# Sign and factor of the converted weights: two GpSimd multiplies against one on VectorE

## The chip, the core and the metric

The kernel runs on one core of a Trainium2 chip. A core has a matrix engine (TensorE, "PE" in the profile, its weight loads "PEld"), a vector engine (VectorE, "DVE"), an activation engine (ScalarE, "ACT"), a general engine (GpSimd, "POOL") and SyncE ("SP"), which here only issues transfers. Every engine works through its own list of instructions in order; a semaphore makes an instruction wait for another engine. The metric is the device time of one execution in microseconds (us).

## The reference

Top-k attention over 8 batches and 8 heads, with 576 positions and a head width of 64, followed by a block with a layer norm and two matrix products. Only the 32 largest scores of each row are kept:

```python
scores = scale * np.matmul(q, k.transpose(0, 1, 3, 2))
kth = np.partition(scores, -top_k, axis=-1)[..., -top_k:-top_k + 1]
scores = np.where(scores >= kth, scores, -1e9)
attn = softmax(scores)                 # written out in the reference
x = attn @ v                           # then (B,H,S,D) -> (B, S, H*D)
xn = (x - mean) / sqrt(var + 1e-6) * g_ln
out = x + maximum(xn @ w_ch1, 0) @ w_ch2
```

The weights w_ch1 (512 x 2048) and w_ch2 (2048 x 512) come in 64-bit floating point, so the kernel reads each of them as two 32-bit words and makes a 32-bit float of them itself; all else is 32-bit.

## The kernel before, in words

**Units and steps.** The attention is cut into 160 units: 128 rows of queries of a pair of heads (or 64 left-over rows), with all 576 keys. The main loop (lines 1263 to 1418) has one step per unit. In step n, VectorE picks the 32nd largest score of unit n. TensorE makes the scores of unit n+2, and ScalarE copies them out of PSUM. For unit n-1, whose threshold is there, ScalarE makes a mask (L532), GpSimd subtracts the scores from it (L535) and ScalarE takes the exponential (L543). The weighted values and the matrix products of finished blocks of rows fill TensorE in between.

**Selection.** `halve` (L447) folds a unit's 576 scores into the larger (L461) and the smaller (L462) of each pair of halves. `select(u, i)` for i = 0 to 3 takes the eight largest (MAX8, L483) of the larger half and replaces them by a very small number (MATCH_REPLACE8, L469); `select(u, 1)` also takes the eight largest of the smaller half (L475). After `select(u, 3)`, the last maximum, the threshold is known. In the kernel before, `halve` of the next unit follows the last maximum.

**Weights.** A `Piece` (L123) is 128 x 512 weights: 16 pieces of w_ch1, and 16 of w_ch2. It is fetched by SyncE (L148, 512 KB), and split (L150): ScalarE takes the absolute value of the upper word (L164), GpSimd clamps it (L165), ScalarE scales the lower word (L166) and takes the sign (L169); for w_ch1 GpSimd multiplies the row's factor from `gcol` into the sign (L171). In the next step VectorE shifts the bits of the upper word left by three (L177), GpSimd adds the lower word (L183) and multiplies by the sign (L185), which writes the finished weight.

**When pieces are converted.** `batches` says which pieces are split in which step: four ahead of step 0, one in each of steps 0 to 7, none in step 8, one in step 9, two in each step from 10 to 18, and the last one in step 19. `join_weights` makes the adds and multiplies a step later: at the end of the step up to step 8, where it also finishes one of the first four pieces, and near its start, behind the masks, from step 9 on. `weights` issues the fetches and the splits, from step 9 on at the end of the step. `ready` keeps the step in which a piece was finished.

**Matrix work.** A block of rows is given to the queue `todo` when its attention is done (the first in step 9). `fill` takes as much from it, eight times in a step, as `slot` allows: while weights are converted (`CONVERTING`), what VectorE's planned time of the step leaves beside TensorE's, and later an even share of what is open. An item whose weights are not ready is left for a later step. The order of all instructions is written out by this program; no scheduler changes it. Scores, transposes and values share five PSUM buffers ("ps"), matrix products have three ("mm").

Of the kernel before, what the change touches and what calls it, by code (L numbers as in the profile page):

```python
# [10 lines left out]
ALU = mybir.AluOpType  # L11
FP32 = mybir.dt.float32
# [17 lines left out]
def compute(  # L30
# [12 lines left out]
    nc = tc.nc  # L43
# [4 lines left out]
    NC, NF = DM // P, DFF // P  # L48
# [65 lines left out]
    half, gcol = columns[:, 0:J], columns[:, J : J + NC]  # L114
# [8 lines left out]
    class Piece:  # L123
# [26 lines left out]
        def split(self):  # L150
            i = self.i
            high = self.raw[:, :, 1].bitcast(FP32)
            if i < 3 * NC:
                self.size = hpool.tile([P, DM], U32, tag="h", name="size")[:]
                self.low = wt_rows[:, i % 8]
                homes = ((opool, "o"), (opool, "o"), (rpool, "r"), (rpool, "r"), (xtpool, "xT"))
            else:
                self.size = wt_rows[:, 2 * i % 8].bitcast(U32)
                self.low = wt_rows[:, (2 * i + 1) % 8]
                homes = ((opool, "o"), (opool, "o"), (rpool, "r"))  # L160
            pl, tag = homes[i % len(homes)]
            self.sign = pl.tile([P, DM], FP32, tag=tag, name="sign")
            size_f = self.size.bitcast(FP32)
            nc.scalar.activation(size_f, high, AF.Abs)  # L164
            nc.gpsimd.tensor_scalar(size_f, size_f, HIGH_MAX, HIGH_MIN, ALU.min, ALU.max)  # L165
            nc.scalar.activation(  # L166
                self.low, self.raw[:, :, 0], AF.Copy, bias=2.0, scale=2.0**-51
            )
            nc.scalar.activation(self.sign[:], high, AF.Sign)  # L169
            if self.i < NF:  # L170
                nc.gpsimd.tensor_scalar(  # L171
                    self.sign[:], self.sign[:], gcol[:, self.c : self.c + 1], 1.0,
                    ALU.mult, ALU.mult,
                )

        def shift(self):
            nc.vector.tensor_scalar(  # L177
# [3 lines left out]
        def join(self):  # L181
            size = self.size
            nc.gpsimd.tensor_tensor(size, size, self.low.bitcast(U32), ALU.add)  # L183
            size = size.bitcast(FP32)
            nc.gpsimd.tensor_tensor(self.dst, size, self.sign[:], ALU.mult)  # L185
            ready[self.i] = now[0]


# [12 lines left out]
    batches = {}  # L201
    queue = list(pieces)
    for n in range(-1, NF + 4):
        count = 4 if n < 0 else 1 if n < NF // 2 else 0 if n == NF // 2 else 1 + (n > 9)
        batches[n], queue = queue[:count], queue[count:]
    batches = {n: x for n, x in batches.items() if x}
    assert not queue
# [3 lines left out]
    def weights(n, phase):  # L211

        now, coming = batches.get(n, []), batches.get(n + 1, [])
        if phase == 0:
            for x in coming if n < LATE else []:
                x.fetch()
            for x in now[0::2] if n < LATE else []:
                x.split()  # L220
        elif phase == 1:
            for x in now if n >= LATE else now[1::2]:
                x.split()
            for x in coming if n >= LATE else []:
                x.fetch()

    def join_weights(n):
        for x in batches.get(n - 1, []):
            x.join()
# [8 lines left out]
    def pop():  # L238
        kind, cost, run, may = todo.pop(0)
        assert not may or may()  # L240
        owed[0] -= cost
        run()
# [30 lines left out]
    def fill(least=0):  # L273
        tick[0] += 1
        loads.settle(LOAD_AGE)
        sends.settle(SEND_AGE)
        ends_later.settle(END_AGE)
        fetch_forms(FETCH_AGE)
        owed[0] = min(owed[0] + share[0], 6.0)
        while todo and (not todo[0][3] or todo[0][3]()):  # L280
            if owed[0] < todo[0][1] / 2 and least <= 0:
                break
            least -= 1
            pop()
# [162 lines left out]
    def halve(u):  # L447

        nt = len(u.tiles)
        u.lo = lopool.tile([P, 2, HALF], FP32, tag="lo", name="lo")
        u.hi = hi_homes[u.i % 2]
        sides = int(doubt is not None)
        u.low, u.body = (sides * LOWS + HALF, sides * LOWS) if doubt is None or u.i // 2 % 2 else (0, LOWS)
        a, b = u.sc[:, 0:nt, 0:HALF], u.sc[:, 0:nt, HALF:S]
        lo, hi = u.lo[:, 0:nt], u.hi[:, 0:nt, u.body : u.body + HALF]  # L460
        nc.vector.tensor_tensor(hi, a, b, ALU.max)  # L461
        nc.vector.tensor_tensor(lo, a, b, ALU.min)  # L462

    def select(u, i):

        nt = range(len(u.tiles))

        def replace(m, t, x):
            nc.vector.match_replace(x, m[:, t, :], x, LOWEST)  # L469

        if i == 1:
            for r in range(low_rounds):
                o = u.low + 8 * r
                for t in nt:
                    nc.vector.max(u.hi[:, t, o : o + 8], u.lo[:, t])  # L475
                if r < low_rounds - 1:
                    for t in nt:
                        replace(u.hi[:, :, o : o + 8], t, u.lo[:, t])
        r0, width = (min(u.low, u.body), HALF + LOWS) if i > 1 else (u.body, HALF)
        pl = brief_small if i in (1, 2) else small  # L480
        m = pl.tile([P, 2, 8], FP32, tag=f"m{i}", name=f"m{i}")
        for t in nt:
            nc.vector.max(m[:, t, :], u.hi[:, t, r0 : r0 + width])  # L483
        if i < TOP_K // 8 - 1:
            for t in nt:
                replace(m, t, u.hi[:, t, r0 : r0 + width])
        if i == 0:
            u.top = m
        u.thr = m
# [47 lines left out]
    def weigh(u, t):  # L537
        g = u.group
        if g.den is None:
            g.den = denpool.tile([P, 2 * J + 1], FP32, tag="den", name="den")  # L540
        col = 2 * u.qt + t
        u.weighed += 1
        nc.scalar.activation(  # L543
            u.e[:, t], u.e[:, t], AF.Exp, bias=u.bias[:, t : t + 1], scale=-scale,
            accum_out=g.den[:, col : col + 1],
        )
        if u.rest:
            den = g.den[:, 2 * J : 2 * J + 1]
        elif u.weighed == 2 and u is [x for x in g.units if not x.rest][-1]:
            whole = [qt for qt in g.qts if qt < J]  # L550
            den = g.den[:, 2 * whole[0] : 2 * whole[-1] + 2]
            g.sums = den
        else:
            return
        nc.scalar.activation(den, den, AF.Copy, bias=DEN_EPS)
# [170 lines left out]
    class Block:  # L726
# [163 lines left out]
        def seven(self):  # L890
# [47 lines left out]
            def evacuate(k):  # L938
# [16 lines left out]
                def join():  # L955
# [8 lines left out]
                    if k == 5:  # L964
                        self.finish(0)

                joined[k] = sums_later.add(join)
                self.ends.append(joined[k])

# [86 lines left out]
    def fetch_forms(age):  # L1056
        if done(formed[0]):
            free = 4 + sum(tick[0] - x >= age for x in used)
            while fetched[0] < min(free, 8 * (len(blocks) - PLAIN)):
                fetch_form()  # L1060
# [96 lines left out]
    def at(i):  # L1157
        return units[i] if 0 <= i < N else None
# [104 lines left out]
    for n in range(END):  # L1263
# [8 lines left out]
        u, nxt, mk = at(n), at(n + 1), at(n - 1)  # L1272
# [34 lines left out]
            brings.pop(n)()  # L1307
        if u:
            select(u, 0)
        for x in batches.get(n - 1, []) if n else []:  # L1310
            x.shift()
        if n > NF // 2:
            join_weights(n)
        if quick:
            for den in recips.pop(n):
                nc.vector.reciprocal(den, den)
# [58 lines left out]
            parts[1]()  # L1375
        if u:
            select(u, 2)
        for blk, i in rows_of.pop(n, []):
            blk.stats(i)
        for blk in gives.get(n - 2, []):  # L1380
# [11 lines left out]
        if mk and len(mk.tiles) > 1 and mk.i >= EARLY:  # L1392
            weigh(mk, 1)
        fill()
        if u:
            select(u, 3)
        if nxt:
            halve(nxt)
        if n == 0:
            for x in batches[-1]:  # L1400
                x.shift()
            for x in batches[-1][:2]:
                x.join()
        weights(n, 1)
        if 0 < n <= NF // 2:
            join_weights(n)
            for x in batches[-1][n + 1 : n + 2]:
                x.join()
        if g and not quick and g.job.hp == NHP - 1:
            for qt in g.qts:  # L1410
                if qt < J:
# [17 lines left out]
@with_exitstack  # L1429
def kernel(  # L1430
    ctx: ExitStack,
    tc: tile.TileContext,
    *operands: bass.AP,
):
    nc = tc.nc
    doubt = ctx.enter_context(tc.tile_pool(name="doubt", bufs=1)).tile(
        [1, 1], I32, tag="doubt", name="doubt"
    )
    compute(tc, *operands, low_rounds=1, doubt=doubt[:])
    again = nc.values_load(  # L1440
        doubt[:], min_val=0, max_val=1,
        skip_runtime_bounds_check_because="a comparison's result",
    )
    with tc.If(again > 0):
        compute(tc, *operands, low_rounds=2, doubt=None)
# [31 lines left out]
```

## Time and profile before

| | us |
|---|---|
| median of the runs (lowest to highest) | 1571.86 (1570.28 to 1573.63) |
| profiled execution | 1571.11 |
| its span | 1569.2 |
| TensorE busy | 1469.0 |
| VectorE busy | 1363.4 |
| ScalarE busy | 1083.8 |
| GpSimd busy | 981.2 |

The page gives busy times, then the span in 40 equal slices of 39 us with the busy share in tenths. A group's row has its line, engine and operation, the tiles, their shapes and the count; behind the first bar the busy time in us and the mean of one in ns; behind the second the idle time of the engine in front of it, with what ended it. A row of the timeline begins with the start and the duration in us. A duration includes the time in which an instruction that has begun is held up. VectorE's and ScalarE's instructions overlap a little, so that the next starts up to 0.1 us before the end of one.

### The profile page before, as it was taken

What the parts mean: (1) busy time and instruction counts of PE and PEld (TensorE: products, weight loads), DVE (VectorE), ACT (ScalarE), POOL (GpSimd) and SP (SyncE); (2) the same over time, 40 slices, a digit from 0 to 9 for tenths busy, and PEclk for the clock granted to TensorE, in tenths of its full rate; (3) what the DMA queues carried; (4) which work ended last, traced back from release to release, by engine and by line L of the source; (5) the groups of instructions that cost most, each with busy time, mean ns of one, the idle gap of its engine ahead of it and who ended that gap; (6) DMA issues with size and microseconds to landing.
All of it is one profiled execution on the core that took longest, in us unless ns stands there. A gap on an engine that the chain in (4) does not pass through costs nothing. (4 is left out here: it accounts for less than half of the span.)

```text
span 1569.2 us, 27215 instructions
## 1 busy us (share of the span) xinstructions
PE 1469.0 (94%) x8046; PEld 1108.0 (71%) x8046; DVE 1363.4 (87%) x3873; ACT 1083.8 (69%) x3081; POOL 981.2 (63%) x1318
## 2 busy tenths in 40 slices
PE   4568889999999999999999999999999998999997
PEld 3346446566787677778777777777777776788886
DVE  7997999899979998999988999999999999768000
ACT  6978887786777767767768676768676776555421
POOL 6968995747465565756566647474746475737524
PEclk9779989999999999999999999999999999999999
DMA  6623551466728865577754687657677557454511
GB/s 170 167 85 97 137 139 53 124 178 181 226 83 194 202 208 153 168 199 153 216 148 134 174 200 197 173 150 191 175 201 206 162 164 208 121 166 125 150 35 50
DMA packets 374774, 245.60 MB, mean 157 GB/s; under 512 B 255956, under 2 KB 343512, under 8 KB 374616
## 3 DMA queue, kind: packets, MB, share of 16 engines
q1 hardware_dynamic: 371048, 243.17, 57.6%
q8 instruction: 67, 1.10, 0.3%
q10 hardware_dynamic: 3568, 0.59, 0.3%
q14 instruction: 91, 0.75, 0.2%
HBM read 166.14 MB, written 77.53 MB: 155 GB/s over the span
## 5 line engine op out<-in xcount | busy, mean ns | idle before, releaser
L535 POOL TENSOR_TENSOR e<-e,sc 128x576 f32<-128x576 f32 x288 | 416.0, 1462 | 453.8 <-ACT e L532 392.9
L819 PE MATMUL hps<-xT,w 128*128 128x256 f32 x2304 | 542.2, 384 | 2.4 <-ACT xT L781 2.4
L819 PEld LDWEIGHTS hps<-xT,w 128*128 128x128 f32 x2304 | 423.0, 191 | 82.2 <-issue 27.2
L483 DVE MAX8 m<-hi 128x8 f32<-128x296 f32 (+1 forms) x1152 | 471.3, 444 | 1.2
L469 DVE MATCH_REPLACE8 hi<-m,hi 128x288 f32<-128x288 f32 (+1 forms) x864 | 377.0, 441 | 0.0
L979 PE MATMUL ops<-w,h 128*128 128x256 f32 x1280 | 304.8, 383 | 1.4 <-ACT o L944 1.4
L979 PEld LDWEIGHTS ops<-w,h 128*128 128x128 f32 x1280 | 233.6, 190 | 44.3 <-issue 13.5
L419 ACT COPY sc<-scps 128x288 f32<-128x288 f32 x576 | 188.5, 402 | 78.5 <-POOL e L535 56.2
L543 ACT ACTIVATE e<-e,m 128x576 f32<-128x576 f32 x288 | 225.1, 784 | 14.6 <-POOL e L535 12.5
L532 ACT ACTIVATE e<-sc,m 128x576 f32<-128x576 f32 x288 | 209.4, 769 | 0.0
L842 ACT ACTIVATE h<-hps 128x512 f32<-128x512 f32 x144 | 86.7, 602 | 114.1 <-PE hps L819 113.5
L577 DVE STREAM_TRANSPOSE sc<-e 128x1152 f32<-128x1152 f32 x87 | 118.8, 1366 | 52.5 <-ACT e L543 46.3
L669 PE MATMUL av<-pt,vb 128*64 128x256 f32 (+2 forms) x1280 | 148.8, 376 | 9.5 <-DMA pt<-turned 7.7
L462 DVE TENSOR_TENSOR lo<-sc 128x576 f32<-128x576 f32 (+1 forms) x160 | 136.1, 850 | 0.0
L461 DVE TENSOR_TENSOR hi<-sc 128x576 f32<-128x576 f32 (+1 forms) x160 | 130.0, 812 | 3.0 <-ACT sc L419 3.0
L669 PEld LDWEIGHTS av<-pt,vb 128*64 128x64 f32 x1280 | 81.6, 140 | 66.4 <-issue 17.1
L438 PE MATMUL scps<-kT,late_qT 64*128 64x288 f32 (+3 forms) x832 | 121.7, 410 | 0.2 <-ACT pt L618 0.2
L979 PE MATMUL ops<-wt,s 128*128 128x256 f32 x512 | 119.4, 383 | 0.0
L475 DVE MAX8 hi<-lo 128x8 f32<-128x288 f32 x288 | 117.5, 443 | 0.0
L438 PE MATMUL scps<-kT,qT 64*128 64x288 f32 x512 | 92.6, 460 | 23.5 <-DVE qT L366 8.0
L606 PE MATMUL tp<-ident,e 128*128 128x128 f32 x456 | 74.2, 290 | 39.9 <-ACT e L543 28.9
L979 PEld LDWEIGHTS ops<-wt,s 128*128 128x128 f32 x512 | 94.7, 190 | 17.3 <-issue 4.4
(111 smaller groups left out, 1793.5 us busy)
## 6 DMA issues: line engine op xcount, KB each, us to landing
turned<-sc SPq DMA_DIRECT2D x87, 576.0 KB, 4.2
pt<-turned SPq DMA_DIRECT2D x348, 144.0 KB, 3.2
w<-forms SPq DMA_DIRECT2D x128, 256.0 KB, 4.7
vb<-in_v_dram SPq DMA_DIRECT2D x80, 288.0 KB, 4.2
raw<-in_moe_w_ch_dram SPq DMA_DIRECT2D x32, 512.0 KB, 4.5
kT<-kept SPq DMA_DIRECT2D x48, 288.0 KB, 3.7
kept<-kT SPq DMA_DIRECT2D x32, 288.0 KB, 3.6
kqin<-in_k_dram SPq DMA_DIRECT2D x116, 72.0 KB, 2.6
```

The costliest lines, as they stand in the source:

```text
L419: nc.scalar.copy(u.sc[:, t, s * HALF : (s + 1) * HALF], u.made[s][t][:, 0:HALF])
L438: nc.tensor.matmul(ps[i * R : i * R + ql, o : o + width], qT[r, q0 : q0 + ql], kT[r, k0 : k0 + width], start=True, stop=True,)
L461: nc.vector.tensor_tensor(hi, a, b, ALU.max)
L462: nc.vector.tensor_tensor(lo, a, b, ALU.min)
L469: nc.vector.match_replace(x, m[:, t, :], x, LOWEST)
L483: nc.vector.max(m[:, t, :], u.hi[:, t, r0 : r0 + width])
L532: nc.scalar.activation(u.e[:, t], u.sc[:, t], AF.Relu, bias=u.edge[:, t : t + 1], scale=-STEEP)
L535: nc.gpsimd.tensor_tensor(u.e[:, t], u.e[:, t], u.sc[:, t], ALU.subtract)
L543: nc.scalar.activation(u.e[:, t], u.e[:, t], AF.Exp, bias=u.bias[:, t : t + 1], scale=-scale, accum_out=g.den[:, col : col + 1],)
L669: nc.tensor.matmul(av[h * D : (h + 1) * D, 0 : g.nq], vb[:, h * (J + 1) + c, :], heads_of(g, h, 0, g.nq // 32)[:, :, c], start=(c == 0), s ...
L819: nc.tensor.matmul(ps[0][:, side * N : (side + 1) * N], w1[:, c, f * P : (f + 1) * P], self.xT[:, c, 0:N], start=(c == 0), stop=(c == NC - 1),
L979: nc.tensor.matmul(bank[name][:, 0:Q], a(j), rhs, start=first and j == 0, stop=(j == G - 1), skip_group_check=not first,)
```

## The change

The factor and the sign are no longer multiplied in by GpSimd: a new function `sign_it` makes one VectorE operation of both, (size x factor) x sign, and writes the finished weight. It comes after `select(u, 2)` of the step behind the split. The four pieces ahead of step 0 are shifted, added and multiplied in step 0 in place of steps 0 to 3. From step 4 on two pieces are split in a step, and the last two in step 15 in place of one in step 19. `halve` of the next unit moves in front of `select(u, 3)`, in all steps.

```diff
             nc.scalar.activation(self.sign[:], high, AF.Sign)
-            if self.i < NF:
-                nc.gpsimd.tensor_scalar(
-                    self.sign[:], self.sign[:], gcol[:, self.c : self.c + 1], 1.0,
-                    ALU.mult, ALU.mult,
-                )
...
         def join(self):
             size = self.size
             nc.gpsimd.tensor_tensor(size, size, self.low.bitcast(U32), ALU.add)
-            size = size.bitcast(FP32)
-            nc.gpsimd.tensor_tensor(self.dst, size, self.sign[:], ALU.mult)
+
+        def sign_it(self):
+            factor = gcol[:, self.c : self.c + 1] if self.i < NF else 1.0
+            nc.vector.scalar_tensor_tensor(
+                self.dst, self.size.bitcast(FP32), factor, self.sign[:], ALU.mult, ALU.mult
+            )
             ready[self.i] = now[0]
...
-        count = 4 if n < 0 else 1 if n < NF // 2 else 0 if n == NF // 2 else 1 + (n > 9)
+        count = 4 if n < 0 else 1 if n < 4 else 2
...
-        for x in batches.get(n - 1, []) if n else []:
+        for x in batches.get(n - 1, []):
             x.shift()
-        if n > NF // 2:
-            join_weights(n)
+        join_weights(n)
...
         if u:
             select(u, 2)
+        for x in batches.get(n - 1, []):
+            x.sign_it()
...
+        if nxt:
+            halve(nxt)
         if u:
             select(u, 3)
-        if nxt:
-            halve(nxt)
-        if n == 0:
-            for x in batches[-1]:
-                x.shift()
-            for x in batches[-1][:2]:
-                x.join()
         weights(n, 1)
-        if 0 < n <= NF // 2:
-            join_weights(n)
-            for x in batches[-1][n + 1 : n + 2]:
-                x.join()
```

## The prediction

> **What bounds the kernel now.** I read the page's busy shares and its 40 slices first, then a table of stretches, then the groups of VectorE and GpSimd in the stretch that the change touches, and last single steps in the timeline.
>
> ```profile
> span 1569.2 us, 27215 instructions
> PE 1469.0 (94%) x8046; PEld 1108.0 (71%) x8046; DVE 1363.4 (87%) x3873; ACT 1083.8 (69%) x3081; POOL 981.2 (63%) x1318
> ...
> PE   4568889999999999999999999999999998999997
> ...
> DVE  7997999899979998999988999999999999768000
> ...
> POOL 6968995747465565756566647474746475737524
> ```
> ```profile
> core 0: us, PE busy (x) PEld busy (x) DVE busy (x) ACT busy (x) POOL busy (x), PEclk, DMA share, GB/s
> 40.00:80.00 40.00, 23.18 (x121) 15.57 (x121) 38.27 (x103) 36.18 (x99) 38.67 (x35) 0.72 0.59 162
> ...
> 160.00:200.00 40.00, 33.12 (x137) 17.46 (x134) 39.82 (x101) 35.56 (x92) 35.85 (x33) 0.91 0.58 152
> 200.00:240.00 40.00, 33.47 (x133) 17.22 (x132) 39.76 (x103) 32.87 (x87) 36.36 (x35) 0.89 0.46 117
> ```
> ```profile
> 240.00:1345.00 1105.00, 1083.79 (x6180) 820.48 (x6180) 1067.97 (x3084) 801.53 (x2349) 667.62 (x940) 1.00 0.64 171
> ```
>
> The run has two regimes. From 240 us on TensorE is busy 98% (1083.8 of 1105), whatever VectorE does. Up to 240 us, the stretch in which the weights are converted, TensorE has holes (23 of 40 us busy, then 33), while VectorE and GpSimd are both full: 38.3 and 38.7 of 40, later 39.8 and 36. The matrix work queued per step is planned and stays the same within about a microsecond from step 22 on (so the order of the two kernels' instructions has it), so an engine change in the first 240 us is worth what it does to the moment at which step 20 ends. After it, TensorE is the limit and hands a delay or a gain through to the end.
>
> In the conversion stretch the groups are these (11.32 us is the first halving, 238.18 us the end of step 20's last maximum):
>
> ```profile
> L462 DVE TENSOR_TENSOR lo<-sc 128x576 f32<-128x576 f32 x21 | 25.3, 1204 | 0.0
> L461 DVE TENSOR_TENSOR hi<-sc 128x576 f32<-128x576 f32 x22 | 24.4, 1110 | 3.0 <-ACT sc L419 3.0
> L177 DVE TENSOR_SCALAR wt<-wt 128x512 uint32<-128x512 uint32 x20 | 18.9, 973 | 9.3 <-POOL wt L165 9.3
> ...
> L177 DVE TENSOR_SCALAR size<-size 128x512 uint32<-128x512 uint32 x12 | 6.4, 543 | 3.6 <-POOL size L165 3.6
> ```
> ```profile
> L185 POOL TENSOR_TENSOR w<-wt,sign 128x512 f32<-128x512 f32 x20 | 27.9, 1394 | 1.6
> L183 POOL TENSOR_TENSOR wt<-wt 128x512 uint32<-128x512 uint32 x20 | 27.0, 1350 | 0.0
> L171 POOL TENSOR_SCALAR sign<-sign,columns 128x512 f32<-128x512 f32 x16 | 17.0, 1065 | 3.4 <-ACT sign L169 1.6 <-ACT m L495 0.8
> L165 POOL TENSOR_SCALAR wt<-wt 128x512 f32<-128x512 f32 x20 | 15.9, 804 | 11.4 <-ACT wt L164 11.1
> ...
> L185 POOL TENSOR_TENSOR w<-size,sign 128x512 f32<-128x512 f32 x12 | 15.9, 1322 | 0.9
> ```
>
> VectorE's own rows hide a loss. Its instructions on two tensors take 0.75 us when GpSimd is quiet and up to twice that beside it; a pair of shifts takes 0.74 us or 2.90 us. Steps without conversion take 7.6 us (245.73 to 253.34), steps with two pieces 11.25 us (171.40 to 182.65):
>
> ```profile
> 11.32 0.76 DVE L461 TENSOR_TENSOR hi<-sc 128x576 f32<-128x576 f32 x1 [3.02 <-ACT sc L419]
> ...
> 171.40 1.20 DVE L461 TENSOR_TENSOR hi<-sc 128x576 f32<-128x576 f32 x1
> 172.53 1.16 DVE L462 TENSOR_TENSOR lo<-sc 128x576 f32<-128x576 f32 x1
> 173.61 0.81 DVE L483 MAX8 m<-hi 128x8 f32<-128x288 f32 x2
> ...
> 175.18 2.90 DVE L177 TENSOR_SCALAR wt<-wt 128x512 uint32<-128x512 uint32 x2
> ...
> 182.65 1.28 DVE L461 TENSOR_TENSOR hi<-sc 128x576 f32<-128x576 f32 x1
> ...
> 197.78 0.74 DVE L177 TENSOR_SCALAR wt<-wt 128x512 uint32<-128x512 uint32 x2
> ...
> 229.21 0.76 DVE L461 TENSOR_TENSOR hi<-sc 128x576 f32<-128x576 f32 x1
> 229.88 0.75 DVE L462 TENSOR_TENSOR lo<-sc 128x576 f32<-128x576 f32 x1
> ...
> 238.18 0.73 DVE L461 TENSOR_TENSOR hi<-sc 128x576 f32<-128x576 f32 x1
> ...
> 245.73 0.73 DVE L461 TENSOR_TENSOR hi<-sc 128x576 f32<-128x576 f32 x1
> 253.34 0.73 DVE L461 TENSOR_TENSOR hi<-sc 128x576 f32<-128x576 f32 x1
> ```
> ```profile
> 171.95 2.20 POOL L165 TENSOR_SCALAR wt<-wt 128x512 f32<-128x512 f32 x2
> 174.85 2.95 POOL L535 TENSOR_TENSOR e<-e,sc 128x576 f32<-128x576 f32 x2 [0.69 <-ACT e L532]
> ```
>
> The two shifts issued at 175.18 are through only when GpSimd's two subtractions are (174.85 + 2.95 = 177.80); the halving at 171.40 was stretched by 0.86 in its two rows beside the clamps. Maxima beside the same subtractions keep their 0.81.
>
> By the Trainium skill (SBUF — State Buffer, "Who interferes with whom") VectorE and GpSimd share one pair of ports under an exclusive lock, taken by a VectorE instruction with two SBUF inputs or in a 2-port mode, and the loser waits for the whole instruction. The 2.90 of the shifts and the undisturbed maxima agree with it.
>
> **The change, part by part.** The sum is over VectorE's way from 11.32 to 238.18 us (226.9 us), since VectorE is the fuller engine there and gets more.
>
> Removed from GpSimd: the 16 factor multiplies (L171, 17.0) and the 32 sign multiplies (L185, 27.9 + 15.9), 60.8 us. With two pieces a step that leaves it the subtractions 2.95, two adds 2.70 and two clamps 1.6, about 7.3 us a step, less than a bare VectorE step. So VectorE's waits for a clamp (9.3 + 3.6) go: **-12.9**.
>
> Added to VectorE: 32 multiplies of sign and factor on 128x512, two tensors in. No row shows that operation; the bounds are 0.37 (half a free pair of shifts, one tensor, 0.74) and 1.20 (a halving row beside GpSimd). I take 0.60, which is the distance between the two halving rows at 229 us (0.67) for 512 columns in place of 576. **+19.2** (11.8 to 38.4).
>
> The shift sits behind the first maxima and replacements of a step, 1.57 us after they begin (173.61 to 175.18). With the halving now in front of the last maximum, that step's first maxima follow the last maximum directly, and so do ScalarE's mask and GpSimd's subtractions:
>
> ```profile
> 1120.32 0.21 ACT L495 ACTIVATE m<-m 128x2 f32<-128x2 f32 x1 [2.08 <-DVE m L483]
> ...
> 1121.42 1.42 POOL L535 TENSOR_TENSOR e<-e,sc 128x576 f32<-128x576 f32 x1 [0.30 <-ACT e L532]
> ```
>
> So the subtractions begin about 1.1 us after the maximum and the shifts come at 1.57, in the middle of the first of them, which is the geometry of 175.18. Where ScalarE is not late, each pair pays 2.90 in place of 0.74; where it is late, 0.74. I take 2.5, nearer to the former, since ScalarE will mostly wait for VectorE: 12 pairs (steps 5 to 16) x 1.76 = 21.1, and four single shifts (steps 1 to 4), held by one subtraction for some 0.9, 3.6: 24.7. Before, the 32 shifts took 25.3, free they are 16 x 0.74 = 11.8, so 13.5 are paid already. **+11.2** (-13.5 to +16).
>
> The halving no longer runs beside the subtractions. Before, 43 rows took 49.7 against 43 x 0.75 = 32.3, so 17.4 of stretch; it stays beside the clamps in half of the 12 two-piece steps, 0.86 each, 5.2. **-12.2** (-17.4 to -7).
>
> Step 0: all four pieces of the first batch are shifted, added and multiplied inside step 0, where they were shifted at its end. ScalarE prepares them one after the other:
>
> ```profile
> 13.59 0.71 ACT L164 ACTIVATE size<-raw 128x512 f32<-128x512 f32 x1
> ...
> 20.31 0.67 ACT L164 ACTIVATE size<-raw 128x512 f32<-128x512 f32 x1
> ```
> ```profile
> 14.24 0.81 DVE L475 MAX8 hi<-lo 128x8 f32<-128x288 f32 x2
> ```
>
> VectorE is ready for them at 14.24, and the fourth is done when ScalarE turns to the fifth piece at 20.31: **+6**. Its chain was hidden before since the joins were spread over steps 0 to 3.
>
> Two pieces a step from step 4: the totals per piece are the same, the steps 17 to 20 become bare, and that is in the counts above. In step 6 ScalarE's sign of the first piece needs the buffer of a piece that VectorE multiplies only after the third maximum of that same step; behind it wait the exponentials and TensorE's transposes. **+2** (0 to 4). SyncE issues two weight loads a step from step 3 in place of one; they are issued a step ahead, so nothing waits. The eight pairs of combined weights that GpSimd forms afterwards come four steps earlier, and no matrix work asks for them sooner.
>
> The halving in front of the last maximum in all other steps: ScalarE gets the threshold some 1.4 us later in a step's order. What hides it is ScalarE's spare time; the cover is not everywhere:
>
> ```profile
> ACT m L495 <- DVE m L483: 81.3, 50, 3.7
> ```
>
> This row of the waits after 240 us says that ScalarE already waits for that maximum 50 times, 81.3 us in all. Each would wait up to 1.4 longer, 0 to 70 us, if all of it reached TensorE; on the other side the halving loses its stretch there too, which VectorE could use only where TensorE is not the limit. I take 0, since TensorE's 98% show that little of the 81.3 reaches it.
>
> Sum: -12.9 + 19.2 + 11.2 - 12.2 + 6 + 2 = **+13.3 us**, on the profiled execution's 1571.1 us (span 1569.2): 1584.4. The median of the runs is 0.75 above that execution, so **1585 us**, 0.8% slower. The single terms give it 1576 to 1597.
>
> **The rivals.** Less than 0.2% (3 us) could not be told from no change.
>
> Faster: GpSimd was the brake, and with 60.8 us less on it the lock costs fade. If ScalarE stays late by 2 us in most steps, the shifts are free as at 197.78: 24.7 becomes some 3, and the sum -8, **1564**. For it: GpSimd's 38.7 of 40. Against it: with VectorE the slower engine ScalarE waits for it, which puts the subtractions onto the shifts. It decides once a pair costs less than 1.4 in place of 2.5. 0.2.
>
> No change: VectorE's delay lies beside TensorE's work. Against it: TensorE has holes in just this stretch. **1572**, 0.1.
>
> Slower still, by the threshold: a third of the 70 us reaches TensorE, **1608**. 0.08.
>
> Slower still, by the ports: each multiply is held by half an add of 1.35, 32 x 0.67 = 21, **1606**. Against it: the adds should be over (1.1 + 2.95 + 2.7 = 6.8 us after the maximum) when the multiplies come at 8. 0.07. The rule of the Trainium skill named above speaks for this one, since the multiply has two SBUF inputs; by it the sum would be 21 us more wherever the two meet.
>
> **How the numbers follow.** Forecast 0.55, and 0.2, 0.1, 0.08, 0.07. Faster 0.2, same 0.1, slower 0.7. The range takes in the faster rival and most of the two dear ones: 1562 to 1604.
>
> **What would show it.** In the changed profile: the multiplies near 0.6 to 0.7 us each; VectorE's waits for clamps gone, a wait of about 6 us for GpSimd in step 0; shift pairs of 2 to 3 us behind the first maxima; two-piece steps of 11 to 12.5 us, bare ones from step 17; step 20 ending near 251 us in place of 238; TensorE at 98% behind it. It is wrong if two-piece steps take under 10.5 us, or if TensorE's idle time after 240 us changes by more than 5 us.

## The result

The changed kernel takes 1588.1 us (median of four runs, 1585.3 to 1591.4) against 1571.1 us for the kernel before in the same session: a ratio of 1.0108, with a 95% interval of 1.0086 to 1.0129, so 13.5 to 20.3 us slower. The forecast was 1585 us, slower. The profiled execution took 1585.3 us (span 1583.5), 2.8 below the median, and 14.2 above the profiled execution of before. Two executions of the runs below were far slower than their others (1732.8 us in run 3, 8455.2 us in run 6); they are in the medians given there, but not in the ratios.

**The profile after.** First the page of the changed kernel, the lines that answer to those of before:

```profile
span 1583.5 us, 27249 instructions
...
PE 1461.5 (92%) x8046; PEld 1103.7 (70%) x8046; DVE 1387.0 (88%) x3905; ACT 1086.1 (69%) x3081; POOL 940.1 (59%) x1270
...
PE   3547889999999999999999998999999998999997
...
DVE  6999999899989998998989999999999999778100
...
POOL 3556667446565665756565747584847575747624
```

GpSimd is 41 us lighter, VectorE 24 heavier, and TensorE does the same 8046 products. Its slices from the sixth on are as before, but for one that is a tenth lower. The table of stretches of the changed kernel, with the columns of the one shown of before:

```profile
40.00:80.00 40.00, 23.16 (x127) 15.60 (x124) 39.79 (x110) 37.79 (x104) 22.97 (x23) 0.83 0.72 192
...
160.00:200.00 40.00, 35.47 (x168) 21.41 (x166) 39.83 (x98) 36.03 (x88) 27.16 (x25) 0.91 0.60 147
200.00:240.00 40.00, 33.05 (x136) 16.85 (x136) 39.93 (x115) 25.84 (x76) 24.27 (x23) 0.92 0.39 92
```

In the conversion stretch VectorE is now full (39.8 to 39.9 of 40) and GpSimd has room (23 to 27, before 36 to 39). The groups of VectorE in the changed kernel, from 10.96 us (first halving) to 249.5 (end of step 20's last maximum):

```profile
L460 DVE TENSOR_TENSOR hi<-sc 128x576 f32<-128x576 f32 x22 | 18.7, 849 | 3.0 <-ACT sc L418 3.0
L172 DVE TENSOR_SCALAR wt<-wt 128x512 uint32<-128x512 uint32 x20 | 18.3, 950 | 1.2 <-POOL wt L165 1.2
L461 DVE TENSOR_TENSOR lo<-sc 128x576 f32<-128x576 f32 x22 | 17.2, 783 | 0.0
...
L182 DVE SCALAR_TENSOR_TENSOR w<-wt,sign 128x512 f32<-128x512 f32 x16 | 13.8, 903 | 1.9 <-POOL wt L178 1.9
L172 DVE TENSOR_SCALAR size<-size 128x512 uint32<-128x512 uint32 x12 | 10.9, 929 | 4.9 <-POOL size L165 4.9
L182 DVE SCALAR_TENSOR_TENSOR w<-size,columns,sign 128x512 f32<-128x512 f32 x12 | 10.3, 893 | 0.2
L182 DVE SCALAR_TENSOR_TENSOR w<-wt,columns,sign 128x512 f32<-128x512 f32 x4 | 4.2, 1078 | 1.2 <-POOL wt L178 1.2
```

The multiplies are the rows of L182: 13.8 + 10.3 + 4.2 = 28.3 us, and 3.1 us of waits for GpSimd's adds in front of four of them. The shifts (L172) take 29.2, the halvings (L460, L461) 35.9. Waits for clamps are down from 12.9 to 6.1. Single rows of VectorE's timeline in the changed kernel show where these come from:

```profile
15.10 0.43 DVE L172 TENSOR_SCALAR size<-size 128x512 uint32<-128x512 uint32 x1 [1.13 <-POOL size L165]
...
18.42 0.76 DVE L172 TENSOR_SCALAR size<-size 128x512 uint32<-128x512 uint32 x2 [2.89 <-POOL size L165]
...
20.09 1.49 DVE L172 TENSOR_SCALAR size<-size 128x512 uint32<-128x512 uint32 x1 [0.91 <-POOL size L165]
...
81.17 2.88 DVE L172 TENSOR_SCALAR size<-size 128x512 uint32<-128x512 uint32 x2
...
87.88 1.40 DVE L182 SCALAR_TENSOR_TENSOR w<-size,columns,sign 128x512 f32<-128x512 f32 x2
...
100.06 2.76 DVE L182 SCALAR_TENSOR_TENSOR w<-wt,columns,sign 128x512 f32<-128x512 f32 x2 [1.21 <-POOL wt L178]
```

The first three carry step 0's wait for ScalarE's and GpSimd's preparation of the first four pieces (1.13 + 2.89 + 0.91 = 4.9 us). The fourth is a pair of shifts beside GpSimd's subtractions, the last a pair of multiplies beside its adds and clamp. GpSimd's timeline in the same trace:

```profile
80.81 2.96 POOL L534 TENSOR_TENSOR e<-e,sc 128x576 f32<-128x576 f32 x2 [2.48 <-ACT e L531]
...
98.75 2.51 POOL L178 TENSOR_TENSOR wt<-wt 128x512 uint32<-128x512 uint32 x2
101.20 1.07 POOL L165 TENSOR_SCALAR wt<-wt 128x512 f32<-128x512 f32 x1
```

The shifts are through at 84.05, just behind the subtractions at 83.77. Two multiplies take 1.40 us at 87.88, where GpSimd is quiet, and 2.76 at 100.06, where the adds last until 101.26 and the clamp until 102.27.

**Where the time was lost.** All runs take the same units in the same order, so the start of a unit's first halving marks how far a run has got. The table gives that start before, and how much later it comes in the other runs, one profiled execution each, in us. The kernels are those of the next section. Where the halving stands in front, the mark comes one maximum (0.8 us) earlier in a step's order, so that for these steps the columns show 0.8 us too little.

| unit | before, at | after | halving behind (1) | halving in front, alone (2) | in front from step 21 (3) | in front to step 16 (4) | multiply alone (8) | multiply left out (6) |
|---|---|---|---|---|---|---|---|---|
| 15 | 171.4 | 15.7 | 14.1 | -1.5 | 0.4 | 13.7 | | -0.2 |
| 20 | 229.2 | 9.6 | 4.0 | -2.2 | 0.4 | 7.7 | 3.9 | -8.6 |
| 30 | 321.0 | 7.0 | 0.4 | -0.5 | 0.5 | 4.0 | 3.8 | -11.1 |
| 100 | 909.3 | 11.7 | 0.9 | 7.8 | 7.9 | 4.1 | 3.9 | -3.3 |
| 155 | 1385.1 | 13.5 | 1.8 | 12.9 | 11.9 | 5.1 | 4.7 | -0.5 |

The changed kernel is 15.7 us late in the middle of the conversion, 7.0 us late at unit 30, and then loses another 6.5 us on the way to unit 155, in a stretch that has no conversion at all. The forecast had all of its +13.3 us in front of unit 21 and nothing behind.

### The profile page after: what moved, and what is told of

The parts are those of the page before. It is cut to its first block, busy times and chain, and to the rows that moved or that the text cites. A ratio compares the mean times of both kernels' runs of the same rounds, so it can differ in the third digit from the quotient of the medians.

```text
span 1583.5 us, 27249 instructions
## 1 busy us (share of the span) xinstructions
PE 1461.5 (92%) x8046; PEld 1103.7 (70%) x8046; DVE 1387.0 (88%) x3905; ACT 1086.1 (69%) x3081; POOL 940.1 (59%) x1270
## 4 chain that ended last, share of the span: by engine, by line
PE 52%; DVE 32%; ACT 8%; DMA 3%; POOL 2%; issue 2%; SPq 1%; ACTq 0%; DVEq 0%; POOLq 0%
PE hps L818 19%; PE ops L978 16%; DVE m L482 9%; DVE hi L468 8%; PE scps L437 5%; PE av L668 4%; DVE sc L576 3%; DVE hi L460 3%; DVE lo L461 3%; DVE hi L474 2%; PE tp L605 2%; PE ops L857 2%; ACT e L531 1%; ACT e L542 1%; ACT sc L418 1%
## 5 line engine op out<-in xcount | busy, mean ns | idle before, releaser
L482 DVE MAX8 m<-hi 128x8 f32<-128x296 f32 (+1 forms) x1152 | 457.5, 442 | 0.3
L576 DVE STREAM_TRANSPOSE sc<-e 128x1152 f32<-128x1152 f32 x87 | 118.9, 1366 | 47.4 <-ACT e L542 41.9
L668 PE MATMUL av<-pt,vb 128*64 128x256 f32 (+2 forms) x1280 | 145.2, 369 | 7.6 <-DMA pt<-turned 4.5
L460 DVE TENSOR_TENSOR hi<-sc 128x576 f32<-128x576 f32 (+1 forms) x160 | 130.5, 815 | 3.0 <-ACT sc L418 3.0
L461 DVE TENSOR_TENSOR lo<-sc 128x576 f32<-128x576 f32 (+1 forms) x160 | 131.7, 823 | 0.0
L668 PEld LDWEIGHTS av<-pt,vb 128*64 128x64 f32 x1280 | 79.9, 138 | 64.4 <-issue 13.5
L605 PEld LDWEIGHTS tp<-ident,e 128*128 128x128 f32 x456 | 59.0, 150 | 93.7 <-ACT e L542 48.2
L494 ACT ACTIVATE m<-m 128x2 f32<-128x2 f32 (+1 forms) x160 | 32.7, 204 | 120.7 <-DVE m L482 120.3
```

The lines of the kernel that those rows point to most:

```text
L668: nc.tensor.matmul(av[h * D : (h + 1) * D, 0 : g.nq], vb[:, h * (J + 1) + c, :], heads_of(g, h, 0, g.nq // 32)[:, :, c], start=(c == 0), s ...
```

## The experiments

**1. Which part costs: the order or the conversion.** In the changed kernel the halving goes back behind the last maximum; all else stays.

```diff
-        if nxt:
-            halve(nxt)
         if u:
             select(u, 3)
+        if nxt:
+            halve(nxt)
```

> The changed kernel with the halving back behind the last maximum. Theory: the shift pairs get freer of the subtractions (at most 12 x 2.1 us), the halvings meet them again (up to 17 us): within 6 us of the changed kernel, 1580 to 1593. Rival, a threshold 1.4 us later reaches TensorE through ScalarE in the 1100 us behind the conversion: 1570 to 1578.

Measured: 1573.9 us, ratio to before 1.0024 [1.0013, 1.0036]. My expectation fell and the rival's came: the changed multiply with its new schedule costs 3.8 us by this ratio, and the order of two operations the rest, some 13 us.

**2. The order alone,** in the kernel before:

```diff
-        if u:
-            select(u, 3)
         if nxt:
             halve(nxt)
+        if u:
+            select(u, 3)
```

> The kernel before with the halving in front of the last maximum, nothing else. Theory: as in the prediction's term taken as 0 after 240 us, and halves against shifts before it: within 5 us of the kernel before, 1567 to 1577. Rival, the later threshold reaches TensorE: 1580 or more.

Measured: 1584.0 us, 1.0078 [1.0061, 1.0095], that is 12 us (9.6 to 14.9) for moving 1.4 us of VectorE's work from behind the last maximum to in front of it. Again the rival's range was the right one. In the table's rows up to unit 30 this run is within 1.5 us of before (the 0.8 us of the mark added), and it loses 13.4 us behind them.

**3 and 4. Where the order costs.** The halving in front only from step 21 on (in the kernel before), and only up to step 16 (in the changed kernel):

```diff
+        if nxt and n > 20:
+            halve(nxt)
         if u:
             select(u, 3)
-        if nxt:
+        if nxt and n <= 20:
             halve(nxt)
```
```diff
-        if nxt:
+        if nxt and n <= 16:
             halve(nxt)
         if u:
             select(u, 3)
+        if nxt and n > 16:
+            halve(nxt)
```

> The kernel before, with the halving in front of the last maximum from step 21 on only. New theory (the later threshold holds ScalarE, whose score copies behind the masks hold PSUM buffers that TensorE needs): the whole loss of the order alone lies here, 1580 to 1586 us. Rival, the loss comes from the conversion stretch: 1569 to 1574.

> The changed kernel with the halving in front of the last maximum up to step 16 only, behind it later. New theory: the conversion's own delay, some 11 us at step 20, is partly given back by unit 30, and nothing is lost behind it: 1573 to 1580. Rival, the prediction's own account (the conversion stretch makes the loss, and TensorE hands it through): 1583 to 1588.

Measured: from step 21 on, 1584.1 us, 1.0076 [1.0056, 1.0096], the same as the order in all steps. Up to step 16, 1577.3 us, 1.0041 [1.0027, 1.0055]. Both times the new theory's range was the right one. So the order costs its 12 us where nothing is converted, and the conversion with the order that I had counted in its sum costs 6.4 us and not 13.3. From 1.0041 to 1.0108, some 10.5 us, is what the later steps add.

Which wait grows is seen in the lists of waits, from 250 to 1350 us for ScalarE and to 1570 us for TensorE (who waited, on whom: us in all, times, the longest). Before, beside ScalarE's 81.3 us for the threshold:

```profile
PE av L669 <- DMA pt<-turned: 7.7, 6, 2.9
PE tp L778 <- ACT sc L419: 3.6, 3, 1.9
PE tp L606 <- ACT sc L419: 3.0, 2, 1.6
PE xo L714 <- ACT oT L687: 2.2, 3, 0.8
```

With the halving in front from step 21 on:

```profile
ACT m L495 <- DVE m L483: 123.1, 65, 5.4
...
PE tp L606 <- ACT sc L419: 11.0, 9, 3.2
PE xo L714 <- ACT oT L687: 5.5, 6, 1.3
PE tp L778 <- ACT sc L419: 4.9, 2, 4.2
PE av L669 <- ACT den L555: 4.3, 3, 1.9
PE av L669 <- DMA pt<-turned: 1.6, 1, 1.6
```

And in the changed kernel:

```profile
ACT m L494 <- DVE m L482: 100.2, 58, 4.5
...
PE tp L605 <- ACT sc L418: 9.3, 8, 3.2
PE xo L713 <- ACT oT L686: 6.4, 9, 1.4
```

ScalarE's wait for the threshold grows by 41.8 us (81.3 to 123.1), and TensorE's three waits on ScalarE's copies (the rows `sc` and `oT`) from 8.8 to 21.4. In the changed kernel these three come to 18.9, and in run 1, which differs from it in the order alone, to 7.4 (1.9 + 3.9 + 1.6). They are not all that moves: in run 3 TensorE also waits 4.3 us for `den` (0.4 before), which ScalarE writes behind the exponentials, and 6.1 us less for the transfers of the turned scores (7.7 to 1.6). What lies between them stands in ScalarE's timeline of the kernel before, behind the threshold's row at 1120.32 that the prediction shows:

```profile
1120.56 1.44 ACT L532 ACTIVATE e<-sc,m 128x576 f32<-128x576 f32 x2
1122.03 1.31 ACT L419 COPY sc<-scps 128x288 f32<-128x288 f32 x4
```

The mask waits for the threshold, and behind the mask in ScalarE's list stand the copies of the next scores out of PSUM. Their values need no threshold, but in this order they come late with it, and TensorE's transposes (L606) wait for the buffers that they free. In 25 waits the copies come later still, when GpSimd's subtractions, which follow the masks, are through:

```profile
ACT sc L419 <- POOL e L535: 56.2, 25, 4.4
```

This row is of the kernel before; run 3 has 49.5 us in 24 waits, so this part did not grow. The stretch from unit 30's to unit 155's first halving, before, in run 3, in the changed kernel and in run 1 (the first figures are the ends, the length and TensorE's busy time; the third busy time is VectorE's):

```profile
320.97:1385.06 1064.09, 1043.69 (x5979) 800.32 (x5979) 1017.02 (x2928) 760.27 (x2237) 640.40 (x933) 1.00 0.66 176
```
```profile
321.47:1396.96 1075.49, 1046.90 (x5980) 801.33 (x5978) 1023.36 (x2928) 760.71 (x2241) 648.99 (x932) 1.00 0.65 174
```
```profile
327.97:1398.56 1070.59, 1043.87 (x5981) 799.25 (x5979) 1023.98 (x2928) 762.49 (x2241) 658.38 (x932) 1.00 0.65 175
```
```profile
321.37:1386.86 1065.49, 1042.51 (x5977) 800.94 (x5977) 1023.75 (x2929) 762.15 (x2237) 641.75 (x933) 1.00 0.66 176
```

Over the same work TensorE idles 20.4 us before, 28.6 in run 3 and 26.7 in the changed kernel. Its busy share falls from 98.1% to 97.3% and 97.5%: less than a point, which the tenths of the page's slices hardly show, is 8.2 of the 11.4 us that run 3 loses in this stretch, and 6.3 of the changed kernel's 6.5. (The rest of run 3's, 3.2 us, stands as busy time of the same 5980 products.) Run 1, with the old order, idles 23.0 us and needs 1.4 us more than before.

A rival for this stretch is VectorE itself, which is nearly as full as TensorE there: its busy time grows from 1017.0 to 1023.4 us in run 3 and to 1024.0 in the changed kernel. Run 1 speaks against it. It has 1023.8 us of VectorE's time too, with the old order, and loses almost nothing.

**5. How the cost grows with the lateness.** In the kernel before, from step 21 on only the first of the two halving instructions stands in front of the last maximum, and the second behind it, so the threshold is 0.7 us late in place of 1.4:

```diff
         nc.vector.tensor_tensor(hi, a, b, ALU.max)
-        nc.vector.tensor_tensor(lo, a, b, ALU.min)
+        u.rest_of_halve = lambda: nc.vector.tensor_tensor(lo, a, b, ALU.min)
...
+        if nxt and n > 20:
+            halve(nxt)
         if u:
             select(u, 3)
-        if nxt:
+        if nxt and n <= 20:
             halve(nxt)
+        if nxt:
+            nxt.rest_of_halve()
```

> The kernel before; from step 21 on only the first of the two halving instructions stands in front of the last maximum, the second stays behind it, so the threshold is 0.7 us late in place of 1.4. Theory (lateness of the threshold): about half of the 12.5 us of the whole swap, 1575 to 1580. Rival, a place in the order as such (a buffer freed or not, the halving beside other work) makes the loss: all or none of it, 1582 to 1586 or 1569 to 1573.

Measured: 1573.7 us, 1.0025 [1.0015, 1.0036], 3.9 us. That is a third of what 1.4 us cost in run 3, and not nothing either: neither expectation was right. The intervals (2.4 to 5.7 us here, 8.8 to 15.1 in run 3) still leave room for a cost in proportion to the lateness. The threshold is waited for no longer than before, and the copies already a little:

```profile
ACT m L495 <- DVE m L483: 82.4, 44, 5.0
...
PE tp L606 <- ACT sc L419: 8.4, 6, 3.2
PE xo L714 <- ACT oT L687: 4.2, 3, 1.8
```

**The copies ahead of the masks,** twice: in the kernel before, and there together with the halving in front. If the copies behind the mask carry the loss, taking them out of its way should free TensorE.

```diff
+        for x in ahead:
+            take_scores(x)
         if mk:
             prepare(mk)
...
-        for x in ahead:
-            take_scores(x)
```

> The kernel before with only the copies of the scores issued in front of the masks. It says what that edit is worth by itself. New theory: the copies waited little for the threshold in the kernel before, so within 5 us, 1566 to 1576, perhaps a little faster. Rival: the masks come 1.2 us later and it is slower, 1577 to 1587.

> The kernel before with the halving in front of the last maximum, and ScalarE's copies of the scores issued in front of the masks. New theory: the copies no longer wait for the threshold, TensorE's buffers come free as before or earlier: 1567 to 1577. Rival, what is late is the mask, the subtraction and the exponential, not the copies: 1581 to 1592.

Measured: 1598.2 us, 1.0164 [1.0141, 1.0188], and with the halving in front 1601.3 us, 1.0181 [1.0163, 1.0199]. Both are slower than anything else here, and than either expectation. Of the kernel before with the copies first, the list of ScalarE's waits says:

```profile
ACT sc L419 <- DMA turned<-sc: 70.4, 27, 4.7
...
ACT sc L419 <- PE scps L438: 42.0, 48, 2.5
...
ACT m L495 <- DVE m L483: 12.6, 15, 1.8
```

A copy that comes earlier finds its target still being read by the transfer of the turned scores, 70.4 us in all (5.6 before), or the scores themselves not made yet, 42.0 us (3.4 before), and now the masks stand behind that. The threshold is hardly waited for any more (12.6 us), and moving the halving costs only another 3 us, within the uncertainty of nothing. That speaks for the copies as the carrier, but it proves it badly, since the run has new and dearer waits in the same place. That the loss passes through the copies and not through the masks and what follows them is thus read from the waits, and not shown by a run.

**6 and 7. The multiply itself.** In the changed kernel the sign and factor are left out (the add writes its result in the weight's place, without them), or go back to GpSimd with everything else as changed:

```diff
         def sign_it(self):
-            factor = gcol[:, self.c : self.c + 1] if self.i < NF else 1.0
-            nc.vector.scalar_tensor_tensor(
-                self.dst, self.size.bitcast(FP32), factor, self.sign[:], ALU.mult, ALU.mult
-            )
             ready[self.i] = now[0]
```
```diff
+            if self.i < NF:
+                nc.gpsimd.tensor_scalar(
+                    self.sign[:], self.sign[:], gcol[:, self.c : self.c + 1], 1.0,
+                    ALU.mult, ALU.mult,
+                )
...
             nc.gpsimd.tensor_tensor(size, size, self.low.bitcast(U32), ALU.add)
+            nc.gpsimd.tensor_tensor(self.dst, size.bitcast(FP32), self.sign[:], ALU.mult)
```

> The changed kernel with the 32 VectorE multiplies of sign and factor left out (the add writes the weight's place; sign and factor are missing from the weights). Theory, VectorE is the limit of the conversion stretch: their 28.3 us of busy time go, and step 20 ends near 225 us in place of 249.5, so 1560 to 1566 us, below the kernel before, since GpSimd's multiplies are gone too. Rival, the way from one maximum over mask, subtraction and add to the next is the limit: at most 8 us go, 1577 to 1588.

> The changed kernel with its new places and two pieces a step, but factor and sign multiplied in by GpSimd as in the kernel before. Theory (the multiply on VectorE costs what its row says): VectorE gives back 28 us, GpSimd gets 61 us; GpSimd then has 2.95 + 2 x (1.35 + 1.4 + 0.8) + 0.9 = 11 us and more a step of two pieces and becomes the limit, so no more than 10 us are won: 1576 to 1590. Rival, VectorE's multiply alone makes the loss and GpSimd had room: 1565 to 1572.

Measured: left out, 1572.8 us, 1.0010 [0.9993, 1.0027], 15 us under the changed kernel and between the two expectations. By the table this run is 11.1 us ahead of before at unit 30 and has lost 10.6 of it by unit 155: here too the order costs its ten microseconds, behind a conversion that ended early. On GpSimd, 1587.4 us, 1.0109 [1.0092, 1.0126], the same as on VectorE and within the theory's range. So the engine that multiplies makes no difference with the rest as changed. The groups of VectorE in the run with GpSimd's multiply (from its first halving to its end of step 20) say why:

```profile
L463 DVE TENSOR_TENSOR lo<-sc 128x576 f32<-128x576 f32 x22 | 30.2, 1372 | 0.0
L462 DVE TENSOR_TENSOR hi<-sc 128x576 f32<-128x576 f32 x22 | 24.2, 1099 | 3.0 <-ACT sc L420 3.0
...
L177 DVE TENSOR_SCALAR wt<-wt 128x512 uint32<-128x512 uint32 x20 | 14.0, 732 | 11.8 <-POOL wt L165 11.8
...
L177 DVE TENSOR_SCALAR size<-size 128x512 uint32<-128x512 uint32 x12 | 6.9, 589 | 10.8 <-POOL size L165 10.8
```

VectorE saves the multiplies and their waits (31.4 us) and 8.3 on the shifts, and pays 18.5 more for the halvings and 16.5 more in waits for clamps. These sums leave it 4.7 us; at the end of step 20 it is 2.6 ahead (246.9 in place of 249.5).

**8. The multiply alone:** run 1 with the old schedule of pieces too, so that only the multiply's engine and place, and the early joins, are changed.

```diff
-        count = 4 if n < 0 else 1 if n < 4 else 2
+        count = 4 if n < 0 else 1 if n < NF // 2 else 0 if n == NF // 2 else 1 + (n > 9)
```

> The multiply on VectorE alone: places of shift, add and multiply as in the changed kernel, but the halving behind the last maximum and the pieces in the steps of the kernel before. Theory, the multiply moves little once the conversion's delay is given back behind it, and a longer conversion gives back less: 1572 to 1582. Rival, GpSimd was the brake and the multiply helps: 1560 to 1569.

Measured: 1575.8 us, 1.0034 [1.0021, 1.0046], 5.3 us. The intervals of this and run 1 (1.0013 to 1.0036) overlap, so two pieces a step from step 4 neither help nor hurt by an amount that these runs resolve. The time lies in the theory's range.

**9 and 10. A better version.** Both start from run 1. In one, GpSimd multiplies every second piece from the tenth on; in the other, shift and add come behind the second maximum (`select(u, 1)`), so that the shifts miss GpSimd's subtractions.

```diff
+            if self.i % 2 and self.i > 7:
+                if self.i < NF:
+                    nc.gpsimd.tensor_scalar(
+                        self.sign[:], self.sign[:], factor, 1.0, ALU.mult, ALU.mult
+                    )
+                nc.gpsimd.tensor_tensor(self.dst, self.size.bitcast(FP32), self.sign[:], ALU.mult)
+                ready[self.i] = now[0]
+                return
```
```diff
         if u:
             select(u, 0)
-        for x in batches.get(n - 1, []):
-            x.shift()
-        join_weights(n)
...
         if u:
             select(u, 1)
+        for x in batches.get(n - 1, []):
+            x.shift()
+        join_weights(n)
```

> The changed kernel with the halving behind the last maximum, and from piece 9 on one of each pair of pieces multiplied by GpSimd as in the kernel before, the other by VectorE. Theory (the conversion stretch is worth something once the swap is gone): VectorE gives back 12 x 0.74 us and more where it was held, 1565 to 1572. Rival, the delay of the conversion is given back anyway by unit 30, so nothing is won: 1572 to 1576.

> The changed kernel with the halving behind the last maximum, and the shifts and adds moved from in front of the second maximum to behind it, where the subtractions should be over. Theory, the shared ports cost VectorE: pairs of shifts fall to 0.74 us, up to 12 x 1.3 us at the end of step 20, but the adds come later and the multiplies wait for them: 1566 to 1575. Rival, the waits for the adds take more than the ports gave: 1575 to 1582.

Measured: 1568.5 us, 0.9991 [0.9982, 1.0001], and 1569.3 us, 0.9992 [0.9983, 1.0002]. Each is faster than run 1 by about 0.3%, within its theory's range, and not to be told from the kernel before. The later shifts, by the groups of VectorE in that run (11 to 241 us):

```profile
L172 DVE TENSOR_SCALAR wt<-wt 128x512 uint32<-128x512 uint32 x20 | 12.5, 666 | 0.0
L172 DVE TENSOR_SCALAR size<-size 128x512 uint32<-128x512 uint32 x12 | 6.9, 597 | 2.3 <-POOL size L165 2.3
```

The shifts come down to 19.4 us (24.8 in run 1, 29.2 in the changed kernel), where undisturbed ones would take 11.8; but the multiplies take 31.5 in place of 27.0. What the shifts save in their own rows, the multiplies mostly pay, so these rows alone don't show why the run is 5 us faster than run 1.

## Why the prediction was right or wrong

**Right in time, by two errors that cancel.** The measured 17 us are some 6.4 of conversion (run 4) and some 10.5 of the order behind it. The forecast had 13.3 and 0.

**The halving in front in all other steps: the step that failed.** It read "I take 0, since TensorE's 98% show that little of the 81.3 reaches it". Runs 2 and 3 put 12 us there, and what the changed kernel adds behind step 16 is 10.5. The busy share told what the lateness that was already there had cost, not what more of it would. ScalarE's 81.3 us in 50 waits were the sign that it had no slack there, and the rows for TensorE's waits on copies (8.8 us) are where much of the next microseconds then showed. The rival with this mechanism had it at 23 us and a chance of 0.08. Its mechanism is the one that the runs bear out, at half its price: of 41.8 us of added wait in run 3, some 12 reached the end. That is about the third that the rival had assumed, of an added wait that was well under its bound of 70.

The prediction also read "TensorE is busy 98% (1083.8 of 1105), whatever VectorE does". The same row has VectorE at 1067.97 of 1105, so that two engines were nearly full there, and the order of VectorE's work still mattered.

**"Hands a delay or a gain through to the end": mostly.** The changed kernel's step 20 ended 11.3 us late (249.5 against 238.2; forecast 251), but 2.3 us of that were the next unit's halving (246.41 to 248.69), which the kernel before has still to do at that point. By the table the delay is 9.6 us at unit 20 and 7.0 at unit 30, with the 0.8 us of the mark 10.4 and 7.8. So of the 13.3 us some 60% was left for TensorE to hand on. From unit 30 to unit 155 the delays of runs 1, 4 and 8, which have the old order there, change by 1.4 us at most in the table, as the prediction said. One error was to take the end of step 20 in one order of the two operations against the same event in the other (2.3 us); the rest of the difference was made up between steps 20 and 30.

**The terms of the conversion,** by the groups above, against the sum:

| term | forecast | measured in the changed kernel |
|---|---|---|
| waits for clamps | -12.9, and +6 in step 0 | 12.9 to 6.1, of it 4.9 in step 0 |
| multiplies | +19.2 (11.8 to 38.4) | +28.3, and 3.1 of waits for adds |
| shifts | +11.2 (-13.5 to +16) | +3.9 |
| halvings | -12.2 (-17.4 to -7) | -13.8 |
| step 6, ScalarE's sign buffer | +2 (0 to 4) | one wait of 4.95 us on ScalarE; its share of the stretch is not shown |

The first four rows come to +14.7 (-6.8 + 31.4 + 3.9 - 13.8), where the stretch itself is 11.7 longer (238.5 against 226.9).

The multiplies were mis-sized: by the list of instructions on L182 an undisturbed one takes 0.68 us, 0.74 with the factor's column, in place of 0.60, and those beside GpSimd up to 1.75. The bound of 1.20 came from one row; in the kernel before a halving row reaches 1.88 (at 70.24), more than the "up to twice" of the prediction. The rival that the ports hold them was right in part: 28.3 is 5.6 us over 32 undisturbed ones (16 x 0.68 + 16 x 0.74 = 22.7). I had taken the adds to be over by then; at 100.06 add and clamp were not.

The halvings have the right size for the wrong reason. The prediction read "The halving no longer runs beside the subtractions". With the halving back in its old place they take 33.6 us (run 1) and 34.5 (run 8). In the new place, but without VectorE's multiplies, they take 52.5 (run 2), 47.4 (run 6) and 54.4 (run 7). So it is not the place, and by run 6, where GpSimd doesn't multiply either, not GpSimd's lighter load. What fits is that where VectorE multiplies ahead of them, the multiplies take the meeting with GpSimd's adds and clamps that the halvings took before, as at 100.06, where the halvings behind the multiplies then take 0.75 us each. The +31.4 and the -13.8 belong together.

The shift pairs behave as said where they meet the subtractions (2.88 us at 81.17), but not in every step: 29.2 us, where the sum had 36.5. The rule of the Trainium skill (SBUF — State Buffer, "Who interferes with whom"), that the later of the two blocks until the first is finished, agrees with this pair and with the multiplies at 100.06.

**The bounds set for the profile.** Two-piece steps took 10.7 to 14.3 us, 12.2 in the mean of steps 5 to 16 (forecast 11 to 12.5); the bare ones came from step 17, as said, and the first four took 7.6 to 9.9 us. TensorE's idle time behind the conversion changed by 6.3 us (unit 30 to 155), over the 5 that I had named as the sign of being wrong, and it was that sign. In run 1, with the old order, it changed by 2.6.

**The rivals.** Faster by relief of GpSimd: GpSimd was relieved (27 of 40 us), and VectorE took the place. No change: only runs 9 and 10, with the order as before, come there. The ports: answered with the multiplies above, 5.6 us and 3.1 of waits in place of 21.

**What stays open.** Whether the order's loss passes by the copies alone, which the 4.3 us for `den` in run 3 make doubtful; why run 10 is faster than run 1; and which of the schedule's parts gives the conversion its remaining 6.4 us.

## What to carry to other kernels

When an instruction is moved ahead of one that another engine waits for, look at the list of waits and not at the busy share: an engine that already waits 50 times for that result has no slack in those steps, and everything behind the wait in its queue, whether it needs the result or not, comes late too. An engine that is 98% busy could still lose most of a percent here, and the page's slices hardly showed it. And undo each part of a change alone even when the total fits, since a fitting total here hid two errors of 7 and 10 us.

## What the runs showed of the hardware that was not expected

A threshold 0.7 us late in every step from the 21st costs 3.9 us (2.4 to 5.7), and 1.4 us late 11.9 (8.8 to 15.1); whether the cost grows faster than the lateness, these intervals leave open. The product (a x column) x b on VectorE takes 0.74 us at 128x512 in 32-bit floating point against 0.68 with a constant. The 42 to 44 instructions of the halvings of the conversion took 33.6 to 37.6 us wherever VectorE multiplied ahead of them, and 47.4 to 54.4 wherever it did not, though neither they nor GpSimd's subtractions were changed.
